# Another order for the first 290 steps of a fused attention and mixing kernel

## The chip, the cores and the metric

The kernel runs on one core of a Trainium2 chip. A core has five engines that work side by side, each through its own queue of instructions in order: TensorE (PE in the profile; PEld is its loading of weights), VectorE (DVE), ScalarE (ACT), GpSimd (POOL) and SyncE (SP). Transfers are issued from the queues of SP, ACT and POOL and carried out by 16 DMA engines. The metric is the device time of one execution in microseconds (us); the median over runs is the figure that counts.

## The reference

Eight batches, 8 heads, 576 tokens, head size 64, and 16 "beacon" keys and values that every token may see. Attention is causal over the tokens. Its result, 576 tokens by 512 channels, goes through a low-rank mixing over tokens (rank 32) and then through a two-layer network of width 2048:

```python
k_all = concat([beacon_k, k]); v_all = concat([beacon_v, v])       # 592 keys
scores = scale * q @ k_all.T ; causal mask over the 576 keys
a = softmax(scores) ; x = a @ v_all                                # (8, 576, 512)
h = x.transpose @ U @ V
u = x + h.transpose
out = u + relu(u @ w_ch1) @ w_ch2
```

Inputs and output are float32; the kernel works in float16 with float32 sums.

## The kernel before

The whole work is cut into small steps, and a string, `SCRIPT`, lists them in the order in which they are emitted. `step()` (named in the listing below) turns one word into instructions. Every engine's queue gets its instructions in that order, so the string is the order of every queue, and an instruction that waits holds all that stand behind it on its engine. A word's first letter names the step. Where a copy can be done by several engines, a letter in the word chooses: V for VectorE, A for ScalarE, G for GpSimd.

Heads go in pairs; pair p belongs to batch p // 4, so batch 0 is pairs 0 to 3 and batch 1 is pairs 4 to 7. The steps of a pair:

- `G` (`group`, line 253): q or k of a pair is copied from its load buffer `st` (for batch 0 `stm`, in float32) into `pr`, in an order that TensorE can turn. In batch 0 it also converts the first rows (`first_heads`, line 741) unless an `H` step does that. `GqV3` is q of pair 3 on VectorE. There are three `pr` buffers.
- `T` (`qkT_units`, lines 261 to 265): five transposes on TensorE into one PSUM bank, then two copies to `qT` or `kT` on the engine named.
- `Sa` to `Sd` (`visit`, lines 316 and 321): the four blocks of scores of a pair; matmuls for both heads into two banks, then two exponentials on ScalarE. `Sa3:1` puts one keep-warm matmul ahead.
- `M` (`mask_head`, lines 304 and 306): two minima on VectorE that mask one head's exponentials. It needs all four score blocks.
- `A` (`av_unit`, lines 331, 339, 340): 15 matmuls with the values, then a reciprocal and a product on VectorE into `xb`. It needs M of its head.

The steps of a batch and of the network:

- `X0.0` to `X0.2` (`mix_units`): the mixing of batch 0, after all its A steps. X0.0 makes the rank-32 product and `qts` on VectorE (line 377); the other two make `uT`, with two copies on VectorE and two on ScalarE each (lines 406 and 408).
- `g` (line 529): four matmuls of the first layer on 512 tokens and the relu on ScalarE, partly on VectorE. `g0` are those of the first block of 512 tokens; they need X0.1, X0.2 and the quarter of `w_ch1` that `w10` to `w13` load.
- `P`, `p`, `W`, `F`, `V`, `N`: products and sums of the second layer, in a form with seven products in place of eight, and the like for the first layer in the last blocks.
- `U`: transposes of `uT` by DMA, issued on SP.
- `k`, `q`, `v`, `b`, `w`: loads, all issued on GpSimd. `q1A` is the first half of the heads of q, batch 1.
- `u`, `c`, `e`, `s`: the load of U and V of the mixing, their conversion (three copies), the spreading of V (two matmuls, two copies) and four small copies ahead of it.
- `I1` (`keep_warm`, line 241): a matmul of 512 columns with the identity whose result is not used.

Batch 0's q and k are loaded ahead of the script by `load_first`, in four sets of two heads, on SP and (the first q, and the beacons) ScalarE: k0, k1, q1, k2, q2, k3, q3 in this order. PSUM has eight banks, shared by all steps. The lines that decide what a T copy or a G copy runs on, and how an idle step is made:

```python
elif name == "I":
    keep_warm(pst([P, 512], F32, name="idle"), int(arg))
elif name == "G":
    group(int(arg[2:]), "kq".index(arg[0]), COPY[arg[1]])
elif name == "T":
    qk_of(int(arg[2:]), "kq".index(arg[0]), (COPY[arg[1]], COPY[arg[1]]))
```

Of the kernel before, what the change touches and what calls it, by code (L numbers as in the profile page):

```python
# [27 lines left out]
def kernel(  # L28
# [760 lines left out]
    def step(t):  # L789
# [80 lines left out]
        TqV14 Sd13 Sb13 M12.1 p10.1 p10.2 Sc13 P16.1 b5 U2.2 M13.0 TkA14 v3 A12.1 q5 A12.0 R17 GkA19  # L870
        P15.0 P15.1 p11.2 Sa14 Sd14 Sc14 x12 P17.0 TkV15 M13.1 P13.0 U2.3 A13.0 Sb14 Z16 M14.0 P17.1
        P13.1 GqA19 GqA18 TkV16 TqA16 A13.1 g2.13 g2.10 TqV17 TqV15 M14.1 v4 g2.4 Sa15 k5 Sc15 TkA17
        P14.0 A14.0 P14.1 A14.1 Sd16 GqV20 Sb15 Sd15 M15.1 GkV18 g2.0 x14 Sc16 M15.0 g2.7 g2.5 g2.2
# [5 lines left out]
        TkV20 TkA21 R22 b7 A19.1 g3.7 A19.0 R23 g3.13 g3.8 g3.5 Sa21 Sb21 Sc21 P24.0 P24.1 A18.1 A18.0
        Sb20 U3.3 Sd21 Sa20 M21.1 M21.0 g3.3 g3.2 Sc20 Sd20 X4.0 g3.4 M20.0 k6 GkV24 M20.1 g3.15 GqA26  # L880
        N5 v5 TkV22 g3.12 A21.0 U3.1 A20.0 g3.10 N1 GkA26 g3.1 x17 q7 g3.0 A20.1 TqV22 TqA23 TkV23 g3.6
        g3.14 g3.9 p30.0 p30.2 A21.1 Sc23 GkV25 p31.0 Sb23 GqV25 Sa23 R24 p30.1 x18 P31.0 P31.1 GkV27
        P32.0 P32.1 TkA24 p31.1 Sc22 p31.2 U3.2 k7 Sd22 v6 Sa22 P36.0 P36.1 Sb22 x19 M22.1 Sd23 M23.0
        P35.0 R25 R26 M22.0 P35.1 X4.1 P37.0 P37.1 X4.2 GqV27 TqA24 TqA25 P33.0 U4.1 P33.1 TkA25 P34.0
        R27 g4.0 GqV28 A22.1 TkV26 GkA28 R28 M23.1 g4.11 GqV29 g4.2 g4.6 TqV26 A23.0 g4.10 A23.1 Sd25
        Sc25 A22.0 g4.4 GkV29 R29 Sb25 GkV30 Sa25 M25.0 Sd24 TqV27 P34.1 TkA27 g4.3 U4.3 TkV28 M25.1
        g4.15 g4.13 g4.9 Sc24 Sa24 x21 Sb24 M24.0 U4.2 X5.0 A25.0 M24.1 g4.8 g4.12 U4.0 GqV31 x22 g4.1
        p40.0 p40.1 GqA30 A25.1 g4.7 Sa27 Sb27 A24.1 g4.14 A24.0 g4.5 p41.0 GkV31 Sc27 x23 Sc26 p41.2
        p41.1 Sd26 P41.0 P41.1 Sa26 Sd27 M27.1 Sb26 P45.0 p40.2 P42.0 P42.1 P45.1 TkA29 x20 X5.1 U5.3
        A27.1 R30 TqV29 M27.0 P46.0 P46.1 P43.0 P43.1 g5.13 A27.0 M26.0 M26.1 Sd29 g5.11 X5.2 g5.4 U5.1  # L890
        TqV28 P47.0 g5.2 A26.1 TkA30 x27 P47.1 A26.0 N0 Sb29 Sc29 R31 N4 g5.6 N2 Sb28 Sa29 g5.0 x24
        P44.0 g5.15 TqA30 M29.1 P44.1 x25 Sd28 Sa28 v7 Sc28 M28.1 M28.0 A29.1 g5.7 g5.14 TkV31 g5.1 g5.5
        M29.0 A28.0 g5.3 N3 A28.1 Sb30 TqV31 Sa30 g5.10 A29.0 U5.0 g5.12 g5.9 x29 g5.8 N6 p51.0 p51.2
        X6.0 p50.0 Sb31 Sd30 p50.1 x26 p51.1 Sc31 P51.0 P51.1 Sd31 p50.2 Sc30 M30.0 M30.1 Sa31 M31.0 x28
        U5.2 P52.0 M31.1 P56.0 X6.1 P55.0 A31.1 V6.0 U6.1 V6.2 P56.1 A31.0 x31 P52.1 A30.1 A30.0 V6.1
        x30 P57.0 P55.1 P57.1 X6.2 X7.0 N7 P53.0 P53.1 U6.2 F61.3 X7.2 P54.0 P54.1 F62.3 F61.2 X7.1
        F66.3 F62.2 F61.0 F65.0 V6.3 F65.3 V7.0 F62.0 U7.2 F66.2 F65.1 F67.3 F63.3 F61.1 F66.0 F62.1
        F63.0 F64.3 F66.1 F65.2 F67.2 F71.3 F67.0 F75.0 F67.1 F63.1 U7.0 F71.0 V7.1 F64.0 U7.3 F63.2
        p61.0 V8.0 P61.0 V7.3 F64.2 F64.1 F76.0 F76.3 U7.1 p61.1 U6.3 p60.0 p60.1 p60.2 U6.0 P61.1 P62.0
        P62.1 P65.0 p61.2 P65.1 guard V7.2 P66.0 P66.1 P63.0 P63.1 F75.3 F72.0 F72.3 F75.2 F77.0 F73.0  # L900
        P67.0 P67.1 F73.3 F71.1 F71.2 F72.1 F72.2 F76.1 F76.2 F75.1 V8.2 V8.1 P64.0 P64.1 F77.1 F77.2
        V8.3 F81.0 F74.0 F73.1 F74.1 U8.2 F77.3 p70.0 p70.2 F74.2 sum F73.2 p71.0 P71.0 p70.1 F74.3
        p71.2 F85.1 p71.1 F81.1 P71.1 P72.0 P72.1 F85.3 P75.0 P75.1 P76.0 P76.1 P73.0 P73.1 F82.1 U8.1
        F86.1 F86.0 F82.0 F87.1 F85.0 F83.1 F81.3 F84.1 F87.0 P77.0 P77.1 F81.2 F85.2 F83.0 F86.3 F82.3
        F86.2 F87.3 U8.0 F82.2 F87.2 F83.3 P74.0 F84.0 P74.1 F83.2 p81.0 F84.2 p80.0 p80.1 F84.3 P81.0
        P81.1 U8.3 p81.1 P82.0 p81.2 P82.1 p80.2 | P86.0 P86.1 P85.0 P85.1 P87.0 | P87.1 P83.0 P84.0
        P83.1 P84.1
# [121 lines left out]
```

## Time and profile before

| | before |
|---|---|
| median of 3 runs | 341.4 us (340.95 to 341.75) |
| profiled execution | 341.91 us |
| its span, first to last instruction | 340.3 us |
| TensorE busy | 330.1 us, 97% of the span |
| VectorE busy | 263.4 us, 77% |
| ScalarE busy | 228.3 us, 67% |
| GpSimd busy | 103.6 us, 30% |
| first g step (g0.8) | at 36.85 us |
| X2.0, from where both orders are alike | at 97.32 us |

A row of a timeline gives the start, the time to the end of the group, the engine, the line, the operation, its output and inputs with their shapes, and how many instructions follow one another; in square brackets stands how long the engine had been idle and what ended that. Instructions on an engine overlap a little, so the price of one is read from the distance between starts. Matmuls are pipelined and their ends are modelled: a busy TensorE need not be a TensorE at full rate. In a view by stretches each row is a stretch of time with its length, and then for every engine the busy time and the number of instructions.

### The profile page before, as it was taken

The page shows a single profiled execution, that of the slowest core. Times are in us where ns is not written, and L with a number is a line of the kernel's source. Part 1 is how long each engine was busy: PE and PEld are TensorE (multiplying, and loading weights), DVE is VectorE, ACT ScalarE, POOL GpSimd, SP SyncE. Part 2 cuts the span into 40 slices and gives each one's busy share as a digit, 9 for nine tenths or more (in the row PEclk, how much of TensorE's full clock was granted, in tenths as well). Part 3 has the DMA queues.
Part 4 walks back from the last instruction along what each step waited for, and adds up shares of the span by engine and source line. Part 5 has one row for each costly group of instructions (what it writes and reads, how often), then busy time and mean ns, then how long its engine had stood idle before and what let it go on. Part 6 is the DMA issues. An engine that isn't in the chain of part 4 may idle for free.

```text
span 340.3 us, 8963 instructions
## 1 busy us (share of the span) xinstructions
PE 330.1 (97%) x3527; PEld 227.9 (67%) x3527; DVE 263.4 (77%) x681; ACT 228.3 (67%) x495; POOL 103.6 (30%) x137
## 2 busy tenths in 40 slices
...
GB/s 170 237 188 167 126 184 197 118 127 213 159 163 189 163 203 127 128 148 191 183 95 145 175 174 115 33 161 99 48 63 159 85 13 63 77 3 94 3 80 128
DMA packets 135600, 44.17 MB, mean 130 GB/s; under 512 B 108384, under 2 KB 130912, under 8 KB 135552
## 3 DMA queue, kind: packets, MB, share of 16 engines
q0 software_dynamic: 69008, 17.54, 60.1%
...
q8 instruction: 29, 0.48, 0.6%
q10 hardware_dynamic: 592, 0.34, 0.3%
...
## 4 chain that ended last, share of the span: by engine, by line
PE 84%; DVE 10%; issue 2%; ACT 1%; DMA 1%; ACTq 0%; DVEq 0%
PE gps L529 25%; PE cpY L620 17%; PE cpD L620 9%; PE sps L316 8%; PE po L331 8%; PE cpA L620 4%; PE fpY L566 3%; DVE gT L581 3%; PE idle L241 2%; PE tps L263 2%; PE fpD L566 2%; DVE sT L601 1%; DVE ob L645 1%; DMA sth<-in_beacon_k_dram 1%; PE ups L397 1%
## 5 line engine op out<-in xcount | busy, mean ns | idle before, releaser
L321 ACT ACTIVATE expt<-sps 128x496 f16<-128x496 f32 (+2 forms) x256 | 111.6, 543 | 13.4 <-PE sps L316 11.9
L529 PE MATMUL gps<-uT,w 128*128 128x512 f16 x384 | 91.8, 380 | 0.0
L620 PEld LDWEIGHTS <-gT 128*128 128x128 f16 x576 | 54.6, 98 | 10.5 <-issue 2.3
L529 PEld LDWEIGHTS <-w 128*128 128x128 f16 x384 | 34.3, 98 | 37.1 <-issue 2.4
L587 POOL TENSOR_SCALAR gT<-gT 128x512 f16<-128x512 f16 x12 | 17.8, 1493 | 105.7 <-DVE gT L581 89.1
L620 PEld LDWEIGHTS <-sT 128*128 128x128 f16 x432 | 40.8, 98 | 8.0 <-issue 2.0
L203 POOL DMA_DIRECT2D vs<-in_v_dram x50 | 40.8, 838 | 3.8 <-DMA w<-in_moe_w_ch_dram 1.7
L304 DVE TENSOR_TENSOR expt<-expt,bigmask 128x512 f16<-128x512 f16 x64 | 26.9, 421 | 18.8 <-ACT expt L321 18.8
L331 PEld LDWEIGHTS <-expt 128*128 128x128 f16 (+1 forms) x960 | 35.2, 98 | 8.7 <-DVE expt L304 1.1
L539 ACT ACTIVATE gT<-gps 128x512 f16<-128x512 f32 x48 | 29.3, 618 | 15.4 <-PE gps L529 14.9
L331 PE MATMUL po<-vs,expt 128*128 128x65 f16 (+1 forms) x960 | 37.8, 194 | 0.7 <-DVE expt L304 0.6
L620 PE MATMUL cpY<-wsum,gT 128*128 128x256 f16 x288 | 36.1, 273 | 0.0
L620 PE MATMUL cpD<-w,sT 128*128 128x256 f16 x288 | 35.6, 273 | 0.3 <-DVE sT L601 0.3
L316 PE MATMUL sps<-qT,kT 64*128 64x80 f16 (+4 forms) x384 | 34.3, 284 | 0.2 <-DVE qT L265 0.2
L340 DVE TENSOR_TENSOR xb<-po,rec 128x320 f16<-128x320 f32 x64 | 31.5, 492 | 2.2
L534 DVE SCALAR_TENSOR_TENSOR gT<-gps,gT 128x256 f16<-128x256 f32 x48 | 19.7, 420 | 13.0 <-ACT gT L533 12.9
L109 ACT ACTIVATE hP<-fpY 128x512 f32<-128x512 f32 x24 | 13.7, 597 | 23.1 <-PE fpY L566 22.0
L533 ACT ACTIVATE gT<-gps 128x256 f16<-128x256 f32 x48 | 18.9, 412 | 12.2 <-PE gps L529 11.9
L316 PEld LDWEIGHTS <-kT 64*128 64x128 f16 x384 | 13.8, 94 | 19.8 <-issue 11.1
L645 DVE TENSOR_TENSOR ob<-cpY,ut 128x512 f32<-128x512 f32 (+1 forms) x28 | 18.7, 667 | 5.9 <-PE cpY L620 5.9
L566 PEld LDWEIGHTS <-wf 128*128 128x128 f16 x192 | 18.6, 98 | 3.1 <-issue 0.7
L620 PE MATMUL cpY<-w,gT 128*128 128x256 f16 x144 | 17.7, 273 | 0.0
...
## 6 DMA issues: line engine op xcount, KB each, us to landing
out_dram<-ob SPq DMA_DIRECT2D x16, 512.0 KB, 4.7
st<-in_k_dram POOLq DMA_DIRECT2D x6, 512.0 KB, 8.0
st<-in_q_dram POOLq DMA_DIRECT2D x6, 512.0 KB, 8.3
vs<-in_v_dram POOLq DMA_DIRECT2D x18, 128.0 KB, 7.9
w<-in_moe_w_ch_dram POOLq DMA_DIRECT2D x4, 512.0 KB, 7.5
w<-in_moe_w_ch_dram POOLq DMA_DIRECT2D x2, 1024.0 KB, 12.0
stm<-in_k_dram SPq DMA_DIRECT2D x4, 256.0 KB, 6.0
out_dram<-ob SPq DMA_DIRECT2D x4, 256.0 KB, 2.8
```

What stands on the lines that cost most here:

```text
L203: nc.gpsimd.dma_start(out=dst[a : a + nq[j], j, :, :], in_=src[hs, ds(q0[j], nq[j]), :].rearrange("h p d -> p h d"))
L304: nc.vector.tensor_tensor(out=e4, in0=e4, in1=bigmask, op=ALU.min)
L316: nc.tensor.matmul(ps[i][:, ds(o, w)], kT[hp, c, ds(P * ch, P)], qT[hp, c, ds(qa, w)], start=True, stop=True,)
L321: nc.scalar.activation(out=ex[i][:, ds(PAD + SLOT * g, gw[g])], in_=ps[i][:, 0 : gw[g]], func=AF.Exp, scale=scale)
L331: nc.tensor.matmul(po[:, j, :], ex[0 : nk[c], ds(blk[(c, j)], P)], vs[0 : nk[c], ds(c * H * E + h * E, E)], start=(c == 0), stop=(c == j),)
L340: nc.vector.tensor_tensor(out=xb[:, h // 2, :, ds(D * (h % 2), D)], in0=po[:, :, 0:D], in1=r.broadcast_to([P, NT, D]), op=ALU.mult)
L529: nc.tensor.matmul(g, w1[:, cc, ts(dc, P)], uT[:, cc, ds(ring(t0), 512)], start=(cc == 0), stop=(cc == NCC - 1))
L534: nc.vector.scalar_tensor_tensor(out=gT[:, dc, H2:512], in0=g[:, H2:512], scalar=0.0, in1=gT[:, dc, 0:H2], op0=ALU.max, op1=ALU.subtract,)
L539: nc.scalar.activation(out=gT[:, dc, :], in_=g, func=AF.Relu)
L566: nc.tensor.matmul(ps[:, i, :], a[:, kk, ts(2 * mp + i, P)], b[:, kk, :], start=opens and i == 0 and kk == 0, stop=kk == 1, skip_group_che ...
L620: nc.tensor.matmul(ps[:, i, :], a[:, f, ds(P * i, P)], b[:, f, :], start=opens and i == 0 and f == 0, stop=f == NK - 1, skip_group_check=True,
L645: nc.vector.tensor_tensor(out=out, in0=ps[:, ii, :], in1=other, op=ALU.add)
```

## The change

Only the string is changed. From its start up to X2.0 the steps (273 without the I1) stand in another order; from X2.0 on the words are the same, but for b4, which now follows X2.0, and one I1 less near 145 us. In the changed part:

- 23 of the 37 I1 steps are gone. The keep-warm matmuls of the `Sa` steps stay.
- 36 copy steps name another engine. GqG1, GkG2, GkG5 and cG were on GpSimd; in the new order no copy of this part is.
- v0A and v0B stand ahead of the other loads of GpSimd; k1A moves from the fourth place to behind M2.0 and Sa3; q2 moves forward, ahead of b1 and k1B; w10, w12 and w13 move behind them; k2 moves behind v1A and b2.
- Pairs 0 to 3 take their scores in another sequence (Sa0, Sd0, Sc0, Sb0 in place of Sa0, Sb0, Sd0, Sc0), GqV3 stands ahead of GkV3, M0.0 and M1.0, and cV, s and eV follow A0.0.
- The first g step is g0.3 where it was g0.8; U0.0 and U0.1 move to behind U0.2 and U0.3.

The diff, with the lines in which only the line breaks differ left out:

```diff
@@ -851,60 +851,59 @@
-        B I1 GqA0 HqA0 I1 I1 I1 k1A I1 b1 I1 HkV0 GkV0 TkV0 v0A TqA0 Sa0:3 I1 GqG1 u I1 GkV1 TkV1 GkA4
-        I1 Sb0 I1 I1 I1 TqV1 Sd0 q1A Sc0 I1 M0.0 GkV3 I1 I1 Sa1:2 I1 GqV2 I1 Sb1 M0.1 I1 I1 GkG2 I1 TkA2
-        TqV2 TkA4 I1 q1B I1 w10 v0B w12 GqA4 I1 Sc1 A0.0 TkV3 Sd1 GqV3 I1 A0.1 Sd2 Sb2 Sa2:1 I1 Sc2 M1.1
-        s M1.0 TqV3 GkG5 I1 A1.1 A1.0 Sc3 GqV6 Sa3:1 M2.1 I1 cG I1 I1 GqV5 k1B Sb3 TqV6 I1 Sd3 TqA4 w13
-        M2.0 eA k2 M3.1 M3.0 I1 TqA5 A2.1 A2.0 Sc4 Sa4 TkV5 I1 A3.1 GqA7 I1 I1 A3.0 Sd5 Sc5 GkV7 TqV7
-        X0.0 Sd4 GkA6 I1 X0.2 X0.1 I1 U0.0 Sa5:0 v1A Sb4 Sb5 g0.8 TkA7 GkV9 M5.1 M4.1 GkV11 M4.0 g0.1
-        M5.0 g0.15 g0.0 b2 TkA6 U0.1 GkV8 g0.10 q2 A5.1 A5.0 Sb7 Sa7 Sd7 w11 A4.1 A4.0 g0.11 GqV9 g0.3
-        Sc7 GqV8 M7.1 M7.0 g0.12 Sb6 Sd6 TqV8 TkV9 TkV11 TqV9 g0.2 Sa6:0 GqA11 Sc6 M6.0 v1B g0.14 g0.5
-        M6.1 g0.6 g0.9 A6.0 A7.1 A7.0 TkA8 A6.1 w20 g0.13 p00.0 w21 g0.4 Sc9 Sd8 X1.0 g0.7 p01.0 X1.2
-        X1.1 p01.1 P01.0 GkV10 p00.1 W0 Sd9 U1.1 TqA11 Sb9 Sa8 W4 W5 W1 P02.0 W2 W3 U0.2 v2 W6 P01.1
-        GqA10 Sc8 Sb8 U0.3 M8.1 p00.2 M8.0 P02.1 TkA10 P05.0 Sa9 b3 p01.2 TqA10 P05.1 P06.0 P06.1 A8.0
-        b4 k3 GkA13 A8.1 Sa10 Sc10 M9.1 P03.0 P03.1 q3 q4 P07.0 A9.1 g1.9 g1.8 M9.0 A9.0 W7 Sb11 Sc11
-        g1.2 g1.7 Sb10 Sd10 M10.0 GqV12 GkV12 R12 g1.1 g1.15 GqA14 Sa11 GqV13 R13 GkA14 R14 Sd11 M11.1
-        g1.5 P07.1 g1.3 A10.0 g1.0 TkV12 M11.0 M10.1 g1.6 g1.12 TqA12 GqV16 A11.1 g1.10 TkV13 P04.0 U1.0
-        U1.3 TqA13 GkA15 P04.1 g1.14 A11.0 k4 A10.1 Sa13 Sd12 g1.11 p10.0 g1.4 GqA17 g1.13 Sa12 Sb12
-        Sc12 p11.0 GqV15 X2.0 M12.0 P11.0 GkA17 P11.1 U1.2 X2.1 GkV16 p11.1 R15 P12.0 P12.1 R16 P16.0
...
-        p20.1 Sc18 Sb18 P26.0 P26.1 R21 Sc19 Sd18 Sa19 p21.2 P25.0 P25.1 GkV22 p20.2 I1 Sd19 Sa18 M18.0
...
+        B HqA0 v0A GkV0 GqV0 I1 HkA0 I1 I1 TkA0 TqV0 Sa0:3 I1 GkV1 u TkA1 Sd0 GqV1 GkV2 Sc0 I1 TqA1 v0B
+        GqV2 Sb0 q1A TqV2 Sb1 M0.1 Sc1 Sd1 TkV2 q1B GqV3 GkV3 M0.0 Sa1:2 M1.0 A0.1 I1 I1 A0.0 TkA3 Sa2:1
+        TqA3 M1.1 GqV5 cV s Sd2 A1.1 Sb2 A1.0 GqA7 eV I1 Sc2 M2.0 Sa3:1 I1 k1A I1 M2.1 GkA5 GkA4 GqV4
+        Sd3 q2 I1 TqV4 A2.1 Sc3 TqV5 A2.0 Sb3 M3.0 I1 b1 TkA4 k1B TkA5 TqA7 w10 M3.1 w12 A3.0 w13 I1 Sc4
+        GqV9 v1A A3.1 GqA6 Sd5 TqV9 GkV6 X0.0 Sb5 X0.2 GkV7 X0.1 b2 Sa5:0 TkV6 Sa4 Sb4 g0.3 Sd4 TkV7
+        g0.9 g0.1 M4.1 g0.11 GqA11 TqV6 g0.8 Sc5 M5.0 M5.1 g0.13 g0.15 A5.0 k2 M4.0 w11 A5.1 Sb7 GkV9
+        Sa7 g0.2 Sc7 GkV8 Sd7 M7.0 A4.1 g0.14 A4.0 GqV8 g0.0 g0.10 M7.1 v1B Sa6:0 TkV8 Sb6 p00.0 p00.2
+        Sc6 TkV9 g0.12 U0.2 g0.5 Sd6 M6.0 g0.4 w20 w21 g0.6 U0.3 TqA8 GkV10 GqA10 M6.1 A6.0 TqA11 U0.0
+        U0.1 A7.0 TkA10 A7.1 A6.1 Sd9 Sc9 p00.1 I1 g0.7 TqA10 X1.0 v2 p01.0 p01.2 Sa8 GkV11 k3 X1.2 X1.1
+        p01.1 P02.0 W0 Sd8 q3 W4 Sb8 W1 W5 W6 Sc8 P01.0 P01.1 TkA11 W2 Sb9 Sa9 M8.0 P02.1 P05.0 P05.1
+        M8.1 M9.1 b3 P06.0 P06.1 W3 P03.0 P03.1 A8.0 A8.1 P07.0 Sa10 Sb10 GkV13 Sc10 M9.0 g1.6 g1.13
+        g1.0 GqA12 g1.14 W7 A9.1 GkV14 A9.0 GkA12 R12 Sd11 GqV13 Sd10 g1.7 q4 M10.0 P07.1 Sb11 Sc11 Sa11
+        k4 R13 g1.5 M11.0 TqV12 GqA14 U1.0 g1.10 g1.9 GqV17 U1.1 M10.1 TqV13 g1.4 g1.15 A10.0 g1.1 A11.0
+        P04.0 R14 TkA13 g1.11 g1.12 P04.1 TkV12 g1.3 GkA15 g1.8 M11.1 A10.1 Sd12 Sb12 A11.1 g1.2 Sa12
+        U1.3 p10.0 GqA15 Sc12 Sa13 p11.0 GqA16 X2.0 b4 M12.0 P11.0 GkA17 P11.1 U1.2 X2.1 GkV16 p11.1 R15
+        P12.0 P12.1 R16 P16.0 TqV14 Sd13 Sb13 M12.1 p10.1 p10.2 Sc13 P16.1 b5 U2.2 M13.0 TkA14 v3 A12.1
...
+        TkA19 R20 p21.1 p20.1 Sc18 Sb18 P26.0 P26.1 R21 Sc19 Sd18 Sa19 p21.2 P25.0 P25.1 GkV22 p20.2
+        Sd19 Sa18 M18.0 U3.0 Sb19 M19.0 P27.0 M18.1 M19.1 P23.0 GqV24 GqA22 TqV20 P27.1 x16 P23.1 g3.11
...
```

More of the change, by code (lines that the diff above doesn't have):

```diff
@@ L869 @@
-        Sc12 p11.0 GqV15 X2.0 M12.0 P11.0 GkA17 P11.1 U1.2 X2.1 GkV16 p11.1 R15 P12.0 P12.1 R16 P16.0
[L870 to L873, printed above, removed]
@@ L879 @@
[L879 to L883, printed above, removed]
@@ L884 @@
[L884 to L907, printed above, removed]
+        B HqA0 v0A GkV0 GqV0 I1 HkA0 I1 I1 TkA0 TqV0 Sa0:3 I1 GkV1 u TkA1 Sd0 GqV1 GkV2 Sc0 I1 TqA1 v0B
+        GqV2 Sb0 q1A TqV2 Sb1 M0.1 Sc1 Sd1 TkV2 q1B GqV3 GkV3 M0.0 Sa1:2 M1.0 A0.1 I1 I1 A0.0 TkA3 Sa2:1
```

39 lines of the change are left out of this document (35 added, 4 removed).

## The prediction

> **What bounds the kernel now.** I read the engine shares of the page first, then the busy time by stretches, cut at the first product of the mixing MLP (36.85 us) and at X2.0 (97.32 us), from where both orders are alike; then TensorE's waits; then each engine's timeline from 0 to 42 us.
>
> ```profile
> PE 330.1 (97%) x3527; PEld 227.9 (67%) x3527; DVE 263.4 (77%) x681; ACT 228.3 (67%) x495; POOL 103.6 (30%) x137
> ```
>
> ```profile
> core 0: us, PE busy (x) PEld busy (x) DVE busy (x) ACT busy (x) POOL busy (x), PEclk, DMA share, GB/s
> 5.00:20.00 15.00, 13.86 (x119) 6.92 (x119) 7.54 (x25) 10.72 (x26) 11.80 (x19) 1.00 1.46 220
> 20.00:36.85 16.85, 15.78 (x235) 9.27 (x233) 15.15 (x50) 14.96 (x40) 11.62 (x18) 1.00 1.54 167
> 36.85:97.32 60.47, 60.45 (x668) 37.37 (x666) 45.26 (x127) 48.81 (x116) 26.93 (x35) 1.00 1.49 164
> ```
>
> TensorE is full from 36.85 us on (60.45 of 60.47), so whatever lies there moves the end one for one: the time is when TensorE reaches the first g step, plus the matmuls left, plus any new holes. Before that TensorE looks busy too, but much of it is the keep-warm matmul of I1 and Sa, the 37 that the next view counts between 5 and 36.85 us:
>
> ```profile
> 5.00:20.00 15.00, 8.11 (x23) 2.05 (x23) 1.00 1.46 220
> 20.00:36.85 16.85, 4.91 (x14) 1.20 (x14) 1.00 1.54 167
> ```
>
> In 20 to 36.85 us VectorE (15.15) and ScalarE (14.96) fill nearly the whole 16.85. So these two engines, fed by the loads, set when the first g starts, and not TensorE.
>
> **The change, part by part.**
>
> *I1.* Twenty-three are gone: 36 stand ahead of the first g before, 13 after; one is added behind it and one removed near 145 us, which cancel. Their price on a full TensorE comes from starts that follow one another:
>
> ```profile
> 1.59 2.74 PE L241 MATMUL idle<-ident 128*128 128x512 f16 x6 [1.59 <-POOL ident masks.py:199]
> 15.63 0.82 PE L241 MATMUL idle<-ident 128*128 128x512 f16 x3
> 16.29 0.20 PE L261 MATMUL tps<-ident,hd 80*128 80x80 f16 x1
> 36.85 1.04 PE L529 MATMUL gps<-uT,w 128*128 128x512 f16 x4
> ```
>
> Three take 16.29 - 15.63 = 0.66, so 0.22 each; the first six take 2.74 / 6 = 0.46 each. If TensorE were the bound throughout, 23 x 0.22 = 5.1 us would go; if it only waits in their place, nothing goes. By the stretches above I take nothing for them and look for the new start of the first g on the other engines.
>
> *Copies.* Thirty-six copy steps have another engine letter; four early jobs of GpSimd (GqG1, GkG2, GkG5, cG) go to VectorE. Prices on ScalarE, start to start:
>
> ```profile
> 17.96 0.65 ACT L109 ACTIVATE pr<-st 128x512 f16<-128x512 f16 x1
> 18.48 1.56 ACT L321 ACTIVATE expt<-sps 128x496 f16<-128x496 f32 x4
> ...
> 25.30 3.38 ACT L321 ACTIVATE expt<-sps 128x496 f16<-128x496 f32 x8 [1.63 <-PE sps L316]
> 28.49 0.80 ACT L109 ACTIVATE qT<-tps 128x64 f16<-128x64 f16 x2
> 29.07 0.83 ACT L109 ACTIVATE Vsb<-vps 128x288 f16<-128x288 f32 x2
> ...
> 35.17 1.37 ACT L408 ACTIVATE uT<-ups 128x336 f16<-128x336 f32 x4
> 36.56 2.86 ACT L321 ACTIVATE expt<-sps 128x496 f16<-128x496 f32 x6
> ```
>
> A regroup (G) is 18.48 - 17.96 = 0.52, a score visit (S, two exponentials) (28.49 - 25.30) / 4 = 0.80, a transpose copy (T, two instructions) 0.58, the four uT copies of X0 1.39. On VectorE:
>
> ```profile
> 15.38 0.43 DVE L253 CAST pr<-stm 128x512 f16<-128x512 f32 x1 [0.58 <-DMA stm<-in_k_dram]
> 15.72 0.41 DVE L741 CAST hd<-sth 80x128 f16<-80x128 f32 x1
> 15.86 0.54 DVE L253 CAST pr<-stm 128x512 f16<-128x512 f32 x1
> ...
> 18.85 0.20 DVE L339 RECIPROCAL rec<-po 128x5 f32<-128x5 f32 x1 [1.01 <-PE tps L261]
> ...
> 22.75 0.88 DVE L159 COPY one<-ident 32x32 f16<-32x32 f16 x4
> ...
> 24.00 0.17 DVE L264 COPY qT<-tps 128x64 f16<-128x64 f16 x1
> ...
> 24.70 0.17 DVE L339 RECIPROCAL rec<-po 128x5 f32<-128x5 f32 x1
> ...
> 25.31 0.18 DVE L339 RECIPROCAL rec<-po 128x5 f32<-128x5 f32 x1
> ...
> 25.94 0.28 DVE L253 COPY pr<-st 128x512 f16<-128x512 f16 x1
> 26.14 0.42 DVE L304 TENSOR_TENSOR expt<-expt,bigmask 128x512 f16<-128x512 f16 x1
> ...
> 26.58 0.42 DVE L253 COPY pr<-st 128x512 f16<-128x512 f16 x1
> ...
> 34.11 0.28 DVE L377 CAST qts<-qtp 128x128 f16<-128x128 f32 x1
> ```
>
> A regroup of batch 0 with its head is 15.86 - 15.38 = 0.48, a later one 0.20, T 0.70, A (reciprocal and product) 0.61, M (two minima) 0.44, s 0.88. c and e have no row on VectorE: c lies between 0.28 (one cast, the 34.11 row) and 1.4 (three like the 15.38 row), I take 0.7, nearer to the cast because its three pieces are small; e, two copies of 288 columns, between 0.2 and 1.4 (the f16 regroup and two T steps), I take 0.7.
>
> *Where the new order is gated.* VectorE now has GqV3 ahead of GkV3, M0.0, M1.0 and every A, so it stands there until q of pair 3 has landed, and M0.0 holds TensorE at A0.0, behind which TkA3 and Sa2 queue.
>
> ```profile
> 10.34 0.37 SPq L196 DMA_DIRECT2D stm<-in_q_dram  x1
> ```
> ```profile
> stm<-in_q_dram SPq DMA_DIRECT2D x3, 256.0 KB, 6.9
> ```
>
> Issued at 10.34 and landing after 6.9: 17.2 us. Then two regroups (0.96), M0.0 (0.44), A0.0, TkA3 and Sa2 on TensorE (about 1.3, an estimate from the 0.2 to 0.8 us blocks of its timeline): ScalarE begins Sa2 near 20.0. From there its queue holds, until X0.1 is copied, 11 score visits (8.8), 4 T (2.3), 4 G (2.1) and the uT copies (1.39): 14.6, to 34.6. VectorE from A0.1 (near 18.9, as now) has 8 A (4.9), 5 M (2.2), 4 G (1.1, some take 0.36), 3 T (2.1), c, s and e (2.3): 12.6, to 31.5 at qts, where the kernel now is at 34.11. So ScalarE decides; with the 0.31 that now lie between the end of its uT copies (35.17 + 1.37) and 36.85, the first g starts at 34.9, 1.95 us earlier.
>
> That holds no hand-over at all. VectorE's stretch now, 18.85 to 34.11, is 15.3 us for 8 A, 5 T, 6 M, 4 G and s, by the same prices 4.9 + 3.5 + 2.6 + 1.1 + 0.9 = 13.0: 2.3 over. ScalarE from 25.30 to 36.56 ran without a gap: 0 over. For a queue as tight as the new ScalarE one I take 1.1, the middle, and keep both ends. First g: 36.0, a gain of 0.85.
>
> *Work left behind the first g.* Ahead of it the new order has done one T more and two score visits (c, d) less than the old, so TensorE owes about 0.25 us more behind it (some 0.3 and 0.2 a visit, 0.3 a T: estimates from the blocks of its timeline). Steps further on are only permuted; U0.0 and U0.1 pass to behind U0.2 and U0.3 on SP's queue, long before P01.1 needs them, and cost nothing unless that queue lags by 10 us. Sum: -0.85 + 0.25 = -0.6 us against the profiled execution (341.91), which is 0.5 above the median 341.4: 340.8.
>
> *GpSimd's queue.* v0A and v0B now go first, then q1A, q1B, and only then k1A, q2, b1, k1B, w10, w12, w13; k2 moves behind v1A.
>
> ```profile
> 13.87 0.75 POOL L196 DMA_DIRECT2D st<-in_q_dram  x1
> ...
> 16.63 2.95 POOL L203 DMA_DIRECT2D vs<-in_v_dram  x4
> 20.00 0.82 POOL L203 DMA_DIRECT2D vs<-in_v_dram  x1 [0.42 <-DMA st<-in_q_dram]
> ```
> ```profile
> vs<-in_v_dram POOLq DMA_DIRECT2D x18, 128.0 KB, 7.9
> ...
> w<-in_moe_w_ch_dram POOLq DMA_DIRECT2D x4, 512.0 KB, 7.5
> ...
> st<-in_q_dram POOLq DMA_DIRECT2D x2, 256.0 KB, 6.2
> ```
>
> The issue at 20.00 waits for the transfer issued at 13.87, eight places before it: here eight are in flight. With 2.95 / 4 = 0.74 an issue and 7 to 8 us of landing, q1A goes out near 12 (thirteenth) and lands near 18.5, q1B near 20.3, k1A (seventeenth) goes out near 15 and lands near 22, w10 goes out near 23 and lands near 31. They are wanted by GqV5 at 20.5, GqA7 at 22.9, GkA5 at 25.3, the first g at 35 to 36. Margins of 2 to 5 us, so I charge nothing; without that cover VectorE or ScalarE stands still, and everything queued behind G, the exponentials above all, is late by the same amount.
>
> **The rivals.**
>
> *A gain in full.* ScalarE runs without gaps, as between 25.30 and 36.56 now: -1.95 + 0.25 = -1.7 us, 339.7; if ScalarE also waits less at the start, down to 339. For it speaks that only 4 jobs of GpSimd come back to the two engines; against it, that each M waits for an exponential and each A for an M.
>
> *Loads late (slower).* If the many v packets in front make q1A land 4 us later than I have it, at 22.5, GqV5 holds VectorE 2 us, then c, s and e, on which TensorE stands at the vps matmul ahead of Sc2, so ScalarE too. Price 2 to 3 us: 342.8 to 343.8. It decides from a landing after 21 us. For it speaks the DMA share, 1.46 and 1.54 in the stretches before 36.85.
>
> *Slow TensorE (slower).* The first six I1 take 0.46 each, later ones 0.22, though the clock column says 1.00: TensorE begins at half rate here. With 3 I1 instead of 6 in front and a hole near 12.5 to 14.5 us (TqV2 waits for q of pair 2), the slow rate may last through A0.0 and Sa2: some eight blocks by 0.25 more, 2 us, 342.8. Rate lost until the first g: some 18 us of matmuls doubled from 6 us on, past 42 us: 347. [...]
>
> *Holes behind the first g.* ScalarE comes to it with no lead, and A5.0 wants M5.0, which wants Sc5's exponentials about 1 us before. Another 1 to 1.5 us late there, or k2 late for GkV9 near 44, gives 341.8 to 342.3.
>
> **How the numbers follow.** 0.2% is 0.7 us, about what a measurement of this kernel can tell from no change. Likeliest, 0.42: a first g 0.3 to 1.4 us earlier, 340.1 to 342.0, at 340.8 (of it 0.17 faster, 0.20 same, 0.05 slower). Gain in full 0.20 (faster). Loads late 0.14, slow TensorE 0.12 (both slower). Holes 0.12 (0.02 same, 0.10 slower). Faster 0.37, same 0.22, slower 0.41. The range, 339.2 to 343.8, leaves out half of the full gain's tail and the long slow rate.
>
> **What would show it.** The first g at 35 to 37 us, with ScalarE unbroken from about 20 us; VectorE waiting for stm<-in_q near 17; no wait of a G on st; I1 spacing at 0.22 by 16 us; TensorE without waits to 97. Wrong if TensorE waits after the first g, if a G waits for its load, or if the first g comes before 34 us, which would say that I1 had cost time after all.

## The result and the profile after

| | before | changed |
|---|---|---|
| median of 12 runs each | 341.59 us (340.73 to 343.12) | 339.78 us (339.0 to 343.4) |
| ratio, changed to before | | 0.9953, 95% interval 0.9933 to 0.9973 |
| profiled execution, its span | 341.91 us, 340.3 us | 339.54 us, 337.8 us |
| first g step | 36.85 us | 33.48 us |
| X2.0 | 97.32 us | 94.74 us |

Medians are over all executions; a ratio leaves out those more than 1.5% above the fastest of the same kernel, which are slow and concern only two runs below (two of twelve with k2 ahead of v1A, one of six with v0A held back).

The change makes the kernel 1.8 us faster by the medians (1.6 by the ratio); 0.6 was predicted. The number lies inside the range (339.2 to 343.8), but what happened is the rival "a gain in full" (339.7) and not the case that I held likeliest.

The page's engine shares and the busy time by stretches of the changed kernel, cut at its own first g and X2.0 (after the stretch and its length: busy time of PE, PEld, DVE, ACT and POOL, granted clock, DMA share, GB/s):

```profile
PE 324.3 (96%) x3504; PEld 225.9 (67%) x3504; DVE 264.3 (78%) x687; ACT 227.7 (67%) x497; POOL 100.6 (30%) x129
```

```profile
5.00:20.00 15.00, 12.06 (x131) 6.61 (x132) 10.29 (x38) 11.44 (x31) 12.28 (x18) 1.00 1.59 212
20.00:33.48 13.48, 12.72 (x201) 7.92 (x198) 11.65 (x43) 13.48 (x37) 8.40 (x13) 1.00 1.40 195
33.48:94.74 61.26, 61.03 (x670) 37.64 (x668) 45.48 (x127) 47.92 (x116) 27.04 (x35) 1.00 1.67 174
```

TensorE is still full from the first g on (61.03 of 61.26), so the start of the first g decides, and it comes 3.37 us earlier. The stretch behind it takes 0.79 us more than the 60.47 of before, and from X2.0 to the end of the span they take 242.98 and 243.06: 3.37 - 0.79 - 0.08 = 2.5 us, the difference of the two spans. ScalarE is busy for 13.48 of the 13.48 us ahead of the first g. The first g step on TensorE, and ScalarE's and VectorE's timelines, which say when that began and what came before:

```profile
33.48 1.04 PE L529 MATMUL gps<-uT,w 128*128 128x512 f16 x4
```

```profile
17.73 0.73 ACT L109 ACTIVATE kT<-tps 128x80 f16<-128x80 f16 x2 [0.88 <-PE tps L263]
18.34 1.07 ACT L321 ACTIVATE expt<-sps 128x496 f16<-128x496 f32 x2
...
31.57 1.47 ACT L408 ACTIVATE uT<-ups 128x336 f16<-128x336 f32 x4
```

```profile
11.90 0.43 DVE L253 CAST pr<-stm 128x512 f16<-128x512 f32 x1 [1.68 <-DMA stm<-in_q_dram]
...
15.39 0.42 DVE L253 CAST pr<-stm 128x512 f16<-128x512 f32 x1
...
19.11 0.53 DVE L163 CAST Usb<-small 128x128 f16<-128x128 f32 x2
19.33 0.61 DVE L164 CAST one<-small 32x576 f16<-32x576 f32 x1
19.87 0.38 DVE L159 COPY one<-ident 32x32 f16<-32x32 f16 x4
20.17 0.17 DVE L339 RECIPROCAL rec<-po 128x5 f32<-128x5 f32 x1
```

Sa2 starts on ScalarE at 18.34 and the uT copies end at 31.57 + 1.47 = 33.04: 14.7 us without a gap. VectorE waits for q of pair 2 (the row at 11.90), not for q of pair 3: GqV3 at 15.39 has no wait. The loads of batch 0 came earlier, as SP's row of q of pair 3 and the list of transfers (last column: median us from issue to landing) show:

```profile
8.21 0.59 SPq L196 DMA_DIRECT2D stm<-in_q_dram  x1
```

```profile
stm<-in_k_dram SPq DMA_DIRECT2D x4, 256.0 KB, 4.6
stm<-in_q_dram SPq DMA_DIRECT2D x3, 256.0 KB, 5.9
```

Before, that transfer was issued at 10.34, and the q transfers took 6.9 us. Behind the first g TensorE has one hole. Its row on TensorE, and the pieces of the chain that ended last which lead to it:

```profile
48.73 0.37 PE L316 MATMUL sps<-qT,kT 64*128 64x336 f16 x5 [0.23 <-DVE gT L534]
```

```profile
23.03 12.00 DMA w<-in_moe_w_ch_dram
35.03 0.28 issue
35.32 8.16 DMA st<-in_k_dram
43.48 0.02 issue
43.50 0.30 DVE pr L253
...
47.44 0.90 DVE pr L253
48.34 0.34 DVE gT L534
```

k2, on GpSimd's queue behind w13, v1A and b2, is issued at 35.32 only after one of the w transfers, 12.00 us long, has landed; it lands at 43.48, and GkV9 on VectorE, which has waited 0.27 us for it, starts then. The chain leads through that wait, but it does not make the hole: the mask step at 45.66 starts 12.18 us behind the first g, and 12.17 us in the second profile of the same program (below), which has no hole. The time is lost after that, at the copy of GkV8 (47.36 to 48.34, in the chain from 47.44): it takes 0.98 us, and 0.28 in the second profile. GpSimd issues a load beside it (47.11 to 48.25); whether that stretches the copy is not shown.

### The profile page after: what moved, and what is told of

Its sections match the earlier page's. It is cut to its first block, busy times and chain, and to the rows that moved or that the text cites. A ratio compares the mean times of both kernels' runs of the same rounds, so it can differ in the third digit from the quotient of the medians.

```text
span 337.8 us, 8917 instructions
## 1 busy us (share of the span) xinstructions
PE 324.3 (96%) x3504; PEld 225.9 (67%) x3504; DVE 264.3 (78%) x687; ACT 227.7 (67%) x497; POOL 100.6 (30%) x129
## 4 chain that ended last, share of the span: by engine, by line
PE 76%; DVE 9%; DMA 9%; issue 1%; POOL 1%; ACT 1%; SPq 1%; DVEq 0%; ACTq 0%
PE gps L529 22%; PE cpY L620 17%; PE cpD L620 9%; PE po L331 7%; PE sps L316 7%; PE fpY L566 4%; PE cpA L620 4%; DMA w<-in_moe_w_ch_dram 4%; PE fpD L566 2%; DMA st<-in_k_dram 2%; DMA sth<-in_q_dram 2%; DVE gT L581 2%; DVE ob L645 2%; DVE sT L601 1%; PE fpA L566 1%
## 5 line engine op out<-in xcount | busy, mean ns | idle before, releaser
L539 ACT ACTIVATE gT<-gps 128x512 f16<-128x512 f32 x48 | 29.3, 621 | 15.4 <-PE gps L529 14.6
L316 PE MATMUL sps<-qT,kT 64*128 64x80 f16 (+4 forms) x384 | 35.3, 285 | 0.6 <-DVE qT L265 0.3
L620 PE MATMUL cpY<-wsum,sT 128*128 128x256 f16 x144 | 17.5, 273 | 0.1
```

The lines of the kernel that those rows point to most:

```text
L316: nc.tensor.matmul(ps[i][:, ds(o, w)], kT[hp, c, ds(P * ch, P)], qT[hp, c, ds(qa, w)], start=True, stop=True,)
L539: nc.scalar.activation(out=gT[:, dc, :], in_=g, func=AF.Relu)
L620: nc.tensor.matmul(ps[:, i, :], a[:, f, ds(P * i, P)], b[:, f, :], start=opens and i == 0 and f == 0, stop=f == NK - 1, skip_group_check=True,
```

## The experiments

"Ratio" is always to the kernel before on the same chip, with its 95% interval.

### The kernel before without its I1

```diff
-        ... TkV0 v0A TqA0 Sa0:3 I1 GqG1 u I1 GkV1 TkV1 GkA4 I1 Sb0 I1 I1 I1 TqV1 Sd0 q1A Sc0 I1 M0.0 ...
+        ... TkV0 v0A TqA0 Sa0:3 GqG1 u GkV1 TkV1 GkA4 Sb0 TqV1 Sd0 q1A Sc0 M0.0 ...
```

The 31 I1 behind TkV0 are left out, to X2.0 and beyond.

> The kernel before without the 31 I1 behind its first transposes (the 6 ahead of them stay; 30 of the 31 stand ahead of the first g). Own theory: these I1 only fill waits for VectorE, ScalarE and the loads, so the first g stays within 0.7 us of 36.85 and the time within 0.8 us of the kernel before. Rival, I1 costs time: 30 x 0.22 = 6.6 us or a large part of it goes. Rival, slow TensorE: the half rate lasts beyond 12 us, the 0.4 to 0.6 us blocks stay, and the time is 1 us or more above the kernel before.

Measured: 341.75 us, ratio 0.9989 (0.9972 to 1.0006); first g at 36.66 (36.85 with them). TensorE's timeline and one of the stretches of 4 us of this kernel:

```profile
16.80 0.21 PE L261 MATMUL tps<-ident,hd 80*128 80x80 f16 x1 [2.52 <-DVE hd L741]
...
18.17 1.00 PE L331 MATMUL po<-vs,expt 128*128 128x65 f16 x15
```

```profile
16.00:20.00 4.00, 3.20 (x41) 2.39 (x42) 2.73 (x12) 2.30 (x7) 3.67 (x5) 0.64 1.53 202
```

Where the I1 stood TensorE now waits, for the same copies. After the wait of 2.52 us the granted clock falls (0.64 over 16 to 20 us) and fifteen A matmuls take 1.00 us in place of 0.63. Neither moves the first g: TensorE had that much room. So in the old order the I1 cost nothing, as the prediction's first step said, and at 36.7 us the clock is back (1.00 from 24 us on).

### The changed kernel with I1 put in

```diff
-        ... Sa0:3 I1 GkV1 u TkA1 Sd0 GqV1 GkV2 Sc0 I1 TqA1 v0B GqV2 Sb0 q1A TqV2 Sb1 M0.1 Sc1 ...
+        ... Sa0:3 I1 GkV1 u TkA1 Sd0 I1 GqV1 GkV2 Sc0 I1 I1 TqA1 v0B GqV2 Sb0 I1 q1A TqV2 Sb1 M0.1 I1 Sc1 ...
```

Twenty-three I1, the number that the change took out ahead of the first g, are spread evenly from TkA1 to g0.3.

> The kernel after with 23 I1 added, evenly between TkA1 and the first g. Own theory: TensorE has about 3 us of room in that stretch, so of 23 x 0.22 = 5.1 us some 1 to 3 us show, as a later first g. Rival, I1 costs time in full: 4.5 to 5.1 us. Rival, I1 is free: within 0.5 us.

Measured: 341.44 us, ratio 0.9985 (0.9970 to 1.0000), 1.1 to 1.7 us above the two series of the changed kernel (339.78 and, below, 340.35), which ran on other chips; by the ratios it is 0.9 to 1.1 us, and the intervals just touch. First g at 35.52. From TkA3's copies to the first g it takes 17.62 us instead of 15.75 (33.48 - 17.73), and behind Sa2 ScalarE now waits four times, 0.89 us in all (the last of the four rows):

```profile
34.20 0.63 ACT L408 ACTIVATE uT<-ups 128x240 f16<-128x240 f32 x2 [0.21 <-PE ups L397]
```

In the new order TensorE has less room, so that some 1 to 2 of the bound of 5.1 us are real there, with the I1 in these places. Taking them out was needed for the new order, but by itself (the run above) it brought nothing.

### The changed kernel without its I1

```diff
-        ... TkA0 TqV0 Sa0:3 I1 GkV1 u TkA1 Sd0 GqV1 GkV2 Sc0 I1 TqA1 v0B ... A0.1 I1 I1 A0.0 TkA3 ...
+        ... TkA0 TqV0 Sa0:3 GkV1 u TkA1 Sd0 GqV1 GkV2 Sc0 TqA1 v0B ... A0.1 A0.0 TkA3 ...
```

> The kernel after without the 11 I1 behind its first transposes. Own theory (ScalarE's unbroken queue sets the first g, I1 only fills): the first g stays within 0.5 us of 33.48 and the time within 0.7 us of the kernel after. Rival, slow TensorE: with still fewer I1 blocks at half rate come back after 12 us, they reach ScalarE, and the first g is 1 us or more later.

Measured: 341.38 us, ratio 0.9969 (0.9945 to 0.9992); first g at 35.54. TensorE's timeline and a stretch of 4 us of this kernel:

```profile
24.70 0.40 PE L263 MATMUL tps<-ident,pr 128*128 128x128 f16 x4 [1.92 <-DVE pr L253]
```

```profile
24.00:28.00 4.00, 3.30 (x47) 2.58 (x47) 3.08 (x11) 3.22 (x8) 3.87 (x6) 0.65 1.33 178
```

The wait at 24.70, which is 0.52 us in the changed kernel where I1 fill the rest, is 1.92 here, and the clock falls behind it (0.65 over 24 to 28 us; after the wait near 13 us it had fallen too, to 0.70 over 16 to 20). From TkA3's copies (18.60) to the uT copies (33.63) ScalarE takes 15.0 us instead of 13.84, with a wait of 0.87 for TensorE. So the I1 that stayed seem to do a little work, but the interval of the ratio overlaps that of the changed kernel, so that no loss of time is shown.

### The old place of k1A in the new order

```diff
-        B HqA0 v0A GkV0 GqV0 I1 ... Sa3:1 I1 k1A I1 M2.1 ... I1 b1 TkA4 ...
+        B HqA0 k1A b1 v0A GkV0 GqV0 I1 ... Sa3:1 I1 I1 M2.1 ... I1 TkA4 ...
```

> The kernel after with k1A and b1 put back ahead of v0A on GpSimd's queue, nothing else. Own theory (GpSimd's first loads delay batch 0's loads on SP): the last q load of batch 0 is again issued near 10.3 us instead of 8.2, GqV2 and GqV3 wait for it, the first g comes 1.2 to 2.5 us later than 33.48, and the time is 1 to 2.5 us above the kernel after. Rival (the order of the steps and the engines of the copies made the gain): the first g moves by less than 0.5 us and the time stays.

Measured: 342.23 us, ratio 1.0018 (0.9995 to 1.0040). The whole gain is gone, and the intervals of the two ratios lie apart. SP's and VectorE's timelines:

```profile
10.19 0.38 SPq L196 DMA_DIRECT2D stm<-in_q_dram  x1
```

```profile
16.89 0.43 DVE L253 CAST pr<-stm 128x512 f16<-128x512 f32 x1 [0.19 <-DMA stm<-in_q_dram]
```

q of pair 3 is issued at 10.19 again and wanted at once when it lands (16.89; the prediction had 17.2), and the first g starts at 35.61 (the prediction had 36.0). Up to that landing this is the timeline that I had drawn, brought about by the load order that I had drawn it from. Behind it two errors of the prediction nearly cancel: Sa2 starts at 20.46 (20.0 predicted), and ScalarE's stretch from there to the end of the uT copies has 14.7 us (15.7 with the loss that I had added). And VectorE waits only 0.19 us for q of pair 3. Of the 2.13 us between this first g and the changed kernel's 33.48, 0.81 remains against the second profile of the changed kernel (34.80, next experiment), in which the clock falls as it does here: q of pair 2 is 0.31 later (13.02 against 12.71), and from there to TkA3's copies it takes 0.49 more (6.83 against 6.34), with the 0.19 in it. Behind the first g the stretch takes 61.76 us against 60.74 there, so that more than half of the loss lies there; 0.46 of it is a wait of TensorE for a weight sum on VectorE at 69.52. That sum had waited 1.26 us for its weights, which GpSimd issues at 51.35 (49.05 there), since the other order makes its whole queue later. The rest was not traced further.

### The changed kernel a second time

No edit; another chip.

> The kernel after once more, unchanged, as the neighbour of the next three. All theories: a ratio to the kernel before inside 0.993 to 0.998. Own theory on the first g (it follows the landing of batch 0's loads, which differs a little from execution to execution): the first g between 33.3 and 35.0 us, and 13.8 us from the copies of TkA3 to those of uT on ScalarE, whatever the landing.

Measured: 340.35 us over 7 runs, ratio 0.9958 (0.9943 to 0.9973): the gain holds. The profile differs from the first one, though the program is the same: first g at 34.80 instead of 33.48. VectorE's, TensorE's and ScalarE's timelines, and stretches of 1 us:

```profile
12.71 0.43 DVE L253 CAST pr<-stm 128x512 f16<-128x512 f32 x1 [0.61 <-DMA stm<-in_q_dram]
```

```profile
13.52 0.21 PE L261 MATMUL tps<-ident,hd 80*128 80x80 f16 x1 [1.93 <-DVE hd L741]
```

```profile
19.05 0.72 ACT L109 ACTIVATE kT<-tps 128x80 f16<-128x80 f16 x2 [0.77 <-PE tps L263]
19.66 1.07 ACT L321 ACTIVATE expt<-sps 128x496 f16<-128x496 f32 x2
...
32.88 1.47 ACT L408 ACTIVATE uT<-ups 128x336 f16<-128x336 f32 x4
```

```profile
13.00:14.00 1.00, 0.48 (x7) 0.38 (x9) 0.37 (x3) 0.72 (x2) 1.00 (x2) 0.99 1.66 230
14.00:15.00 1.00, 1.00 (x10) 0.46 (x7) 1.00 (x3) 0.55 (x2) 0.72 (x2) 0.50 1.90 167
15.00:16.00 1.00, 1.00 (x8) 0.63 (x7) 0.38 (x4) 1.00 (x4) 0.00 (x0) 0.50 1.59 195
16.00:17.00 1.00, 1.00 (x4) 0.11 (x2) 1.00 (x4) 0.88 (x3) 0.96 (x2) 0.50 1.66 205
17.00:18.00 1.00, 1.00 (x19) 0.69 (x18) 1.00 (x7) 0.78 (x2) 1.00 (x2) 0.81 1.47 213
```

q of pair 2 lands 0.81 us later than in the first profile (12.71 against 11.90). From there to TkA3's copies it is 6.34 us against 5.83: the granted clock is at half from about 14.0 to 17.4 us, which costs the other 0.5. The other profiles of the new order bear this out: the same way takes 5.87 and 5.98 us where the clock stays at 1.00 (two k copies on VectorE, and with I1 put in), and 6.34 to 6.90 where it falls to 0.50 (without I1, k1A in its old place, k2 ahead of v1A, both edits). From TkA3 on the two are alike: 13.83 and 13.84 us to the uT copies. Behind the first g the stretch takes 60.74 us with no hole, 0.27 more than before; 0.25 was predicted.

### The old order with v0A first

```diff
-        B I1 GqA0 HqA0 I1 I1 I1 k1A I1 b1 I1 HkV0 GkV0 TkV0 v0A TqA0 Sa0:3 ... TkV1 GkA4 I1 Sb0 ... TqV2 TkA4 ...
+        B I1 GqA0 HqA0 I1 I1 I1 v0A k1A I1 b1 I1 HkV0 GkV0 TkV0 TqA0 Sa0:3 ... TkV1 I1 Sb0 ... TqV2 GkA4 TkA4 ...
```

GkA4 is moved behind TqV2, since its load is later.

> The kernel before with v0A ahead of k1A and b1 on GpSimd's queue, and GkA4, which needs k1A, moved from behind TkV1 to ahead of TkA4; nothing else. Own theory (what GpSimd issues first delays batch 0's loads, in the old order too): q of set 3 is issued 1 to 2 us earlier than 10.34, GkV3 no longer waits until 15.4, the first g comes 0.5 to 1.5 us earlier than 36.85 and the time falls by 0.5 to 1.5 us. Rival (the loads matter only in the new order of steps, since VectorE is what binds the old one): the first g moves by less than 0.4 us and the time stays.

Measured: 341.78 us, ratio 0.9985 (0.9962 to 1.0009); first g at 36.34. SP's row of q of pair 3:

```profile
8.46 0.48 SPq L196 DMA_DIRECT2D stm<-in_q_dram  x1
```

The loads of batch 0 are issued as early as in the changed kernel, but the first g gains only 0.5 us. TensorE's rows say where the rest went:

```profile
16.05 0.21 PE L261 MATMUL tps<-ident,hd 80*128 80x80 f16 x1 [0.33 <-DMA hd<-in_beacon_k_dram]
16.70 0.40 PE L263 MATMUL tps<-ident,pr 128*128 128x128 f16 x4 [0.44 <-ACT pr L109]
```

GkV3 on VectorE runs at 13.99, 1.4 us earlier than before (15.38). But TkA4 stands early in the old order, and TensorE waits there for b1 and for the GkA4 that was moved, both late now that v0A goes first; A0.0's reciprocal comes at 18.67, only 0.2 us earlier (18.85). So neither half does it alone: the new order with the old load order gives 1.0018, the old order with the early loads 0.9985, both together 0.9953. What the old order would gain from the early loads with TkA4 further back is not shown.

### Copies back on GpSimd

Two runs. The first puts GqG1, GkG2, cG and GkG5 back, the second leaves out GkG5:

```diff
-        ... TkA1 Sd0 GqV1 GkV2 Sc0 ... GqV5 cV s ... M2.1 GkA5 GkA4 ...
+        ... TkA1 Sd0 GqG1 GkG2 Sc0 ... GqV5 cG s ... M2.1 GkG5 GkA4 ...
```

> The kernel after with GqV1, GkV2, GkA5 and cV on GpSimd, as in the kernel before. Own theory: the four copies are not what made the gain, the first g moves by less than 0.7 us and the time by less than 0.7 us. Rival (GpSimd's copies were the cost, since its load issues queue behind them): GpSimd's loads go out 2 to 3 us later, a G waits for its load, and the time rises by 1.5 us or more.

> The kernel after with GqV1, GkV2 and cV on GpSimd, but GkA5 left on ScalarE. Own theory, now (GpSimd stands at a copy until its load has landed, and every load that it issues later is late): GqG1 and GkG2 wait for batch 0's loads until about 10.8 us, v0B and what follows go out about 4 us later, but the second stand, the 4 us of GkG5 for k1A, is gone; the time is 1 to 4 us above the kernel after, and under the 347.1 of the run with all four. Rival (each GpSimd copy slows VectorE beside it): three of the four copies give three quarters of the loss, 5 us or more.

Measured: 347.1 us, ratio 1.0169 (1.0135 to 1.0203), first g at 40.45; without GkG5 343.05, ratio 1.0031 (1.0009 to 1.0054), first g at 37.51, 2.7 us above the changed kernel on the same chip. GpSimd's and TensorE's timelines of the first:

```profile
8.26 0.71 POOL L253 CAST pr<-stm 128x512 f16<-128x512 f32 x1 [1.61 <-DMA stm<-in_q_dram]
9.26 0.29 POOL L741 CAST hd<-sth 80x128 f16<-80x128 f32 x1 [0.29 <-DMA sth<-in_q_dram]
10.79 0.62 POOL L253 CAST pr<-stm 128x512 f16<-128x512 f32 x1 [1.24 <-DMA stm<-in_k_dram]
...
24.85 0.80 POOL L253 COPY pr<-st 128x512 f16<-128x512 f16 x1 [3.95 <-DMA st<-in_k_dram]
...
27.20 0.54 POOL L193 DMA_DIRECT2D hd<-in_beacon_k_dram  x1
```

```profile
32.39 0.20 PE L261 MATMUL tps<-ident,hd 80*128 80x80 f16 x1 [3.81 <-DMA hd<-in_beacon_k_dram]
```

GpSimd stands at each copy until its load has landed, 1.61 + 0.29 + 1.24 + 3.95 = 7.1 us in these rows (in the kernel before, with k1A loaded early, it stood 0.62 us at GqG1, 0.49 at GkG2 and not at GkG5), and behind the copies stand the issues of v0B, q2, b1, k1B and the w loads. b1 goes out at 27.20 (19.66 in the changed kernel), and TensorE stands 3.81 us at the transposition that needs it. Without GkG5 it goes out at 22.02, and TensorE stands 2.05 us at the same place, where that profile doesn't name what it waited for. I had expected less than 0.7 us from the four copies; the rival had it right. That three of them cost 2.7 and not 5 us or more speaks against the other rival, that each GpSimd copy slows VectorE beside it.

### k2 ahead of v1A

```diff
-        ... Sc4 GqV9 v1A A3.1 ... A5.0 k2 M4.0 ...
+        ... Sc4 GqV9 k2 v1A A3.1 ... A5.0 M4.0 ...
```

> The kernel after with k2 ahead of v1A on GpSimd's queue. Own theory: k2 (issued at 35.32, landing at 43.5) holds GkV9 on VectorE and through it a 0.2 us hole on TensorE at 48.7; the hole goes, the time falls by 0 to 0.5 us. Rival: v1A comes late for A5.0 instead and TensorE waits there, 0.5 us or more slower.

Measured: 341.91 us, ratio 0.9971 (0.9944 to 0.9998), a wide interval (single runs from 339.69 to 347.83). The stretch from the first g (34.82) to X2.0 is 60.75 us with no hole, but the second profile of the changed kernel has none either (60.74). The hole of 0.23 us is not in every execution, and it came from the stretched copy and not from k2 (see the result), so that the expectation had its cause wrong; the edit brings nothing that can be measured.

### Two k copies on VectorE

```diff
-        ... Sa3:1 I1 k1A I1 M2.1 GkA5 GkA4 GqV4 ...
+        ... Sa3:1 I1 k1A I1 M2.1 GqV4 GkV4 GkV5 ...
```

> The kernel after with the regroups of k for pairs 5 and 4 on VectorE instead of ScalarE (GqV4 GkV4 GkV5 in place of GkA5 GkA4 GqV4). Own theory (ScalarE's unbroken queue of 14.7 us sets the first g): 2 x 0.52 us leave it, VectorE has the room, and the first g comes 0.5 to 1.0 us earlier than 33.48; the time falls by as much, if TensorE stays full behind it. Rival (VectorE or the loads are as tight): the first g moves by less than 0.3 us, or later.

Measured: 339.98 us over 7 runs, ratio 0.9926 (0.9897 to 0.9954); first g at 33.98. ScalarE's timeline where the two copies (1.04 us) had stood:

```profile
18.29 0.73 ACT L109 ACTIVATE kT<-tps 128x80 f16<-128x80 f16 x2 [0.39 <-PE tps L263]
...
25.44 2.13 ACT L321 ACTIVATE expt<-sps 128x496 f16<-128x496 f32 x4 [0.61 <-PE sps L316]
...
32.09 1.37 ACT L408 ACTIVATE uT<-ups 128x336 f16<-128x336 f32 x4
```

From TkA3 to uT it takes 13.80 us, as with the copies on ScalarE (13.84). It waits 0.61 us for TensorE instead, and the rest of the 1.04 shows as exponentials that follow one another less closely. So ScalarE does not decide alone: the chain through VectorE and TensorE is as tight. The ratio is the lowest of all, but its interval overlaps that of the changed kernel (0.9953), which ran on another chip, so that no gain over it is shown.

### Both edits, and v0A held back

The last two runs join the two edits above; the second of them also puts a step ahead of v0A, a GpSimd copy of one element that waits for the first k load, so that the v packets don't meet it:

```diff
-        B HqA0 v0A GkV0 GqV0 I1 ...
+        B HqA0 Yk0 v0A GkV0 GqV0 I1 ...
```

> The kernel after with GqV4 GkV4 GkV5 in place of GkA5 GkA4 GqV4, and k2 ahead of v1A. Own theory: the stretch from TkA3 to uT on ScalarE stays near 13.8 us (VectorE and TensorE are as tight as ScalarE), the wait of GkV9 for k2 and the holes near 48 us go, the time is 0 to 0.8 us below the kernel after. Rival: v1A or w11 come late for the first block, 0.3 us or more slower.

> The run before this one with a tiny GpSimd copy ahead of v0A that waits until k of set 0 has landed (Yk0). Own theory (what GpSimd issues first slows batch 0's loads): v0A goes out near 4 us instead of 2.3, q of set 3 is issued at or before 8.2 us and GqV2 runs before 11.9 us, the first g comes 0.2 to 1.0 us earlier than without the hold, the time falls by as much. Rival (v and q1 are then late): A0.1 or GqV5 waits for its load, and the time rises.

Measured: 340.8 us, ratio 0.9971 (0.9949 to 0.9992) for both edits, no better than either; with v0A held back 346.3 us, ratio 1.0105 (1.0070 to 1.0141). The profile of the latter is that of its longest execution, 348.13 us. VectorE's row of q of pair 2, and two rows of TensorE:

```profile
11.06 0.43 DVE L253 CAST pr<-stm 128x512 f16<-128x512 f32 x1 [0.89 <-DMA stm<-in_q_dram]
```

```profile
28.13 0.20 PE L261 MATMUL tps<-ident,hd 80*128 80x80 f16 x1 [1.43 <-DMA hd<-in_beacon_k_dram]
...
45.44 0.42 PE L331 MATMUL po<-vs,expt 128*128 128x65 f16 x5 [2.92 <-DMA vs<-in_v_dram]
```

v0A goes out at 4.69 instead of 2.3. Batch 0's loads are issued no earlier for it (q of pair 3 at 8.69) but land faster: q of pair 2, issued at 6.41, is taken at 11.06, 4.65 us later, against 6.12, 12.28 and 6.16 with both edits alone, and TkA3's copies start at 17.93 against 19.12. So far the theory held. But what else GpSimd issues is later: TensorE waits 1.43 us for b1, so that the first g is at 35.05 (34.96 with both edits), and behind it the A steps of batch 1 wait 4.3 us in three waits for v1A, whose last load goes out at 38.10 (35.96 with both edits). The rival had the time right, but not the places.

The median landing of batch 0's q loads is 6.9 us in the kernel before and 6.6 in the new order with k1A in front, and 5.9 in the changed kernel with v0A in front. From the issue of q of pair 2 to its use it is 6.46 us in the new order with k1A in front (6.56 to 13.02), 5.6 to 6.3 in its nine profiles with v0A in front, and 4.65 in this one with neither. So how fast these loads land goes with what GpSimd issues first, though the case with neither rests on one execution. Why they land later behind k1A than behind v0A is not shown.

## Why the prediction came out as it did

**What bounds the kernel: right.** TensorE is full from the first g on in both profiles of the changed kernel, but for 0.23 us in the first, and everything was won ahead of it.

**I1 at nothing: right for the old order, not for the new one.** The old order without I1 measures 0.9989 (0.9972 to 1.0006). But put back into the new order, 23 I1 cost about 1 us and a first g at 35.52: with the new order taking them out is worth something, and the prediction had nothing for it. The test that I gave, a first g before 34 us, could not tell: it came at 33.48 in one profile and 34.80 in the other of the same program, by the landing of the loads and the clock.

**Copy prices: near enough.** c took 19.87 - 19.11 = 0.76 (0.7 taken). s took 20.17 - 19.87 = 0.30, not 0.88; what stretched the old row is not shown (a cast of GpSimd stands beside it, 22.72 to 23.38). ScalarE's queue from Sa2 to the uT copies held 14.6 us by the prices and took 14.7.

**The gate: wrong.** The step that failed is "Issued at 10.34 and landing after 6.9: 17.2 us". I took the issue time from the profile of before, although the change puts v0A where k1A stood on GpSimd's queue. In the changed kernel the transfer is issued at 8.21, GqV3 waits for nothing, and Sa2 starts at 18.34 and 19.66 in the two profiles (20.0 predicted). What VectorE waits for instead is q of pair 2 (taken at 11.90 and 12.71). Putting k1A and b1 back in front gave back 10.19 and 16.89; that the first g then came at 35.61, close to the 36.0 predicted, is in part luck, since Sa2 started 0.46 later and ScalarE's stretch was 1.0 shorter than predicted.

**Hand-overs: wrong by 1.0 us, the largest mistake in the sum by the second profile.** I took the middle of 0 and 2.3; measured is 14.7 - 14.6 = 0.1 in the first profile, and 32.88 + 1.47 - 19.66 = 14.7 in the second too. In that second profile the first g is at 34.80, where the prediction had 34.9 before this term was added. The end without loss was the one with ScalarE's own row beside it (25.30 to 36.56 without a gap); I should have weighed it by that row instead of taking the middle. From 36.0 to the 34.80 of the second profile it is thus 0.34 for the gate and 1.0 for this term, less 0.14 between the uT copies and the first g; to the 33.48 of the first profile it is 1.66 for the gate, the larger mistake there, 1.0 and 0.13.

**That ScalarE decides: right in the timeline, too strong as a statement.** Taking 1.04 us from it moved nothing (13.80 against 13.84 us), since the chain through VectorE and TensorE has no more room than it.

**Work left behind the first g: right in size.** 0.25 predicted; 0.27 in the second profile, 0.79 in the first. Of the difference 0.23 is the hole at the stretched copy; the other 0.29 was not traced. k2 did come late for GkV9, as the rival "holes behind the first g" had it, but the 0.27 us were made up again on VectorE. With them two signs of being wrong were met, a wait of TensorE after the first g and one of a G for its load, and neither decided anything.

**GpSimd's queue: right in times, incomplete in costs.** q1A was issued at 12.43 (near 12), k1A at 15.80 (near 15), w10 at 21.55 (near 23), and no G waited for its load in the first profile but GkV9, 0.27 us. But the four copies that left GpSimd were priced only as new work on other engines (the prediction says VectorE; GkG5 went to ScalarE, where the sum has it). That GpSimd would stand at them, with the issues of later loads behind, was not named; put back into the new order they cost 2.7 us without GkG5 and some 7 us with it.

**Slow TensorE: the place was right, the price too high.** The prediction had a hole at 12.5 to 14.5 us that waits for q of pair 2, and a slow rate that lasts through A0.0 and Sa2, worth 2 us. The hole is there (1.46 and 1.93 us), and in the second profile a slow rate behind it, for 0.5 us (0.5 to 1.1 over the profiles). It is not the first slow rate lasting: in that profile the small transposes took 0.25 to 0.28 us each up to 9.3 us, 0.20 at 10.86, ahead of the hole, and 0.25 at 15.13.

**The range of the likeliest case** does not follow from its first g: 0.3 to 1.4 us earlier, with 0.25 more behind it, gives 341.4 to 340.2 us and not 342.0 to 340.1. The measured 339.78 and 340.35 lie on either side of its lower end.

The sum by the second profile: -2.05 at the first g, +0.27 behind it, +0.18 from X2.0 to the end, -1.6 us of span (338.7 against 340.3), against -0.85 + 0.25 predicted. The first profile adds an earlier q of pair 2 and no slow rate.
